# Values at the end of each unit, and a last token chunk filled up with zeros, in an attention + MLP-mixer kernel

## The chip, the core and the metric

The kernel runs on one NeuronCore of one Trainium2 chip. The metric is the device time of one execution in microseconds (us), as the median of several runs. Inputs and outputs lie in HBM. The engines work side by side, each through its own queue in program order: TensorE (matmuls, "PE"; its weight loads are "PEld"), VectorE ("DVE"), ScalarE ("ACT"), GpSimd ("POOL"), and SyncE ("SP"), which here only starts DMAs.

## What is computed

Threshold attention over 8 batches of 8 heads, 576 tokens and 64 dimensions per head, followed by one MLP-mixer block (mixing over tokens, then over channels) on the joined heads (576 x 512 per batch). All in float32; the four weights arrive as float64.

```python
# attention, per head
scores = q @ k.T / 8
thresh = max(scores, axis=-1) - tau
scores = where(scores >= thresh, scores, -1e9)
attn   = softmax(scores)                  # (sum + 1e-9)
x      = attn @ v                         # heads joined: (8, 576, 512)
# mixer
h   = relu(x.T @ w_tok1) @ w_tok2         # 576 -> 256 -> 576 tokens
u   = x + h.T
out = u + relu(u @ w_ch1) @ w_ch2         # 512 -> 1536 -> 512 channels
```

## The kernel before

The work on attention is cut into 144 units, 18 for each batch: one unit is 128 rows of scores for two heads (a pair). The 576 tokens are four chunks of 128 and a last one of 64; the last chunks of two pairs share a unit (`SHARED`). For one unit the steps are:

- `scores(u)`: TensorE multiplies with a contraction of 64 (the head's dimensions), head 0 in rows 0 to 63 of the array and head 1 in rows 64 to 127; VectorE takes the maximum; GpSimd makes the bias.
- `weigh(u)`: ScalarE makes the thresholded exponentials and their sums (four activations of 576 columns).
- `norm(u)`, one unit later: GpSimd divides by the sum.
- `turn...(u)`, two units later: transposed weights eT (on TensorE in batch 0; from batch 1 on by VectorE in 32x32 blocks and DMAs).
- `values(b, p, c)`: TensorE multiplies eT with v. Each head uses 64 columns of the array; the result is copied to xT by ScalarE.

```python
# scores: 64 rows of the array for each head
nc.tensor.matmul(sc[h][rows, f, 0:HS], lhsT=qT[r, cols], rhs=kT[r, HS*f : HS*f+HS], ...)   # r = 64 partitions
# values: 128 rows, 64 columns of the array for each head
nc.tensor.matmul(to[r], lhsT=vl[:, r], rhs=eT[:, NI], start=True, stop=False, ...)
for c in range(NI):
    for h in range(2):
        nc.tensor.matmul(to[r], lhsT=lv[:, j, :], rhs=eT[:, j], ...)
nc.scalar.copy(out=x, in_=ps)                            # to xT
```

Once the values of a batch are complete, `push(b)` puts the mixer's steps for it into a list (`todo`). `fill(share)` takes a share of a unit's quota from that list, so that TensorE has full-array work while the softmax of the units goes through the other engines. (`...` marks cuts.)

```python
def token_mlp(b):
    def turn_x(t):                                       # t = 0..4; MT = [128, 128, 128, 128, 64]
        M = MT[t]
        if t == 0:
            s["x"] = work.tile([P, NT, DM], F32, tag="x", bufs=1, ...)
        ...                                              # four transposes on TensorE
        nc.scalar.copy(out=s["x"][0:M, t, :], in_=...)
    def tok1(m):                                         # m = 0, 1
        for t in range(NT):
            M = MT[t]                                    # the last chunk: 64 rows
            nc.tensor.matmul(ps, lhsT=w1[0:M, t, P*m : P*m+P], rhs=s["x"][0:M, t, :], ...)
        nc.scalar.activation(out=s["a"][:, m, :], in_=ps, func=AF.Relu)
    def tok2(c, f): ...                                  # two matmuls; VectorE adds to xT
def channel_mlp(b, uT, i):
    def ch1(j): ...                                      # four matmuls "c", Relu to g on ScalarE
    def ch2(t, part): ...                                # transposes and three matmuls each, then out
```

The main loop, one turn for each unit. `weight(n)` prepares n steps of the mixer's weights (float64 to float32, on ScalarE, VectorE and GpSimd), as long as there are any.

```python
for u in range(len(units) + LAG + 4):
    ...
    if on: scores(u)
    if 0 < u <= len(units): norm(u - 1)
    if b_now: weight(2)
    if back: ...                                         # turn(w) or turn_blocks(w), w = u - 2; values become due
    if b_now: fill(0.4)
    weight(2 if b_now else 1)
    if on: weigh(u)
    if b_now: fill(0.3)
    while due and due[0][0] <= u:
        _, b, p, c = due.popleft()
        values(b, p, c)
        if p == NP - 1 and c == 1:
            push(b)
    if b_now: fill(0.3)
    weight(2 if b_now else 1)
    if on: ...                                           # loads of q, k, v; prep of later pairs
```

Each matmul of float32 operands in the program appears as two passes (two MATMUL records) in the trace.

Of the kernel before, what the change touches and what calls it, by code (L numbers as in the profile page):

```python
# [9 lines left out]
F32 = mybir.dt.float32  # L10
# [7 lines left out]
P = 128  # L18
# [3 lines left out]
def kernel(  # L22
# [26 lines left out]
    nc = tc.nc  # L49
    B, H, S, D = q.shape  # L50
    DM = H * D
# [3 lines left out]
    NI = 4  # L55
    MAIN = NI * P
    LAST = S - MAIN
    NT = NI + 1
    MT = [P] * NI + [LAST]
    NP = H // 2  # L60
# [8 lines left out]
    const = ctx.enter_context(tc.tile_pool(name="const", bufs=1))  # L69
    ld = ctx.enter_context(tc.tile_pool(name="ld", bufs=2))  # L70
    work = ctx.enter_context(tc.tile_pool(name="work", bufs=2))
# [52 lines left out]
    w1 = const.tile([P, NT, DTOK], F32, name="w1")  # L124
    w2 = const.tile([P, NTK, S], F32, name="w2")
    wc1 = const.tile([P, NJ, NCC, P], F32, name="wc1")
    wc2 = const.tile([P, NJ, DM], F32, name="wc2")

# [102 lines left out]
    def need(i):  # L233

        weight(3 * i + 4 - steps_done)
# [35 lines left out]
    def in_blocks(b):  # L271
        return b > 0

    def prep(n):
        lq, lk = loaded.pop(n)
        made = []
        for src, name in ((lq, "qT"), (lk, "kT")):
            sb = work.tile([P, S], F32, tag=name, name=f"{name}_{n}")
            nc.vector.transpose(out=sb, in_=src.rearrange("p n d -> p (n d)"))  # L279
            made.append(sb)  # L280
        heads[n] = made
# [99 lines left out]
    def values(b, p, c):  # L381

        lv, vl = vals[b * NP + p]
        if b not in xTs:
            xTs[b] = xTs[b + 1] = work.tile([P, NP, 2 * S], F32, tag="xT", name=f"xT_{b}")
        key = (b, p - p % 2, c) if c == "s" else (b, p, c)
        n, N, tok = (1, LAST, MAIN) if c == "s" else (2, 2 * P, 2 * P * c)
        first = LAST * (p % 2) if c == "s" else 0
        eT = eTs[key] if c == "s" else eTs.pop(key)
        if in_blocks(b):  # L390
            eT = eT[:, 0 : NK * n * P].rearrange("p (i c x) -> p c i x", i=4, c=NK)
            eT = eT[:, :, first // 32 : first // 32 + N // (32 * n), :]
        else:
            eT = eT[:, 0 : NK * n * P].rearrange("p (c x) -> p c x", c=NK)[:, :, first : first + N]
        ps = ps_tr.tile([P, MAIN], F32, tag="tr", name=f"pv_{b}_{p}_{c}")[:, 0:N]
        to = ps.rearrange("p (i x) -> p i x", x=32 * n) if in_blocks(b) else ps
        for h in range(2):
            r = slice(D * h, D * h + D)
            nc.tensor.matmul(to[r], lhsT=vl[:, r], rhs=eT[:, NI], start=True, stop=False, skip_group_check=True)  # L399
        for c in range(NI):  # L400
            for h in range(2):
                r = slice(D * h, D * h + D)
                j = (NI + 1) * h + c
                nc.tensor.matmul(to[r], lhsT=lv[:, j, :], rhs=eT[:, j], start=False, stop=(c == NI - 1), skip_group_check=True)  # L404
        x = xTs[b][:, p, S * (b % 2) + tok : S * (b % 2) + tok + N]
        if in_blocks(b) and n == 2:
            x = x.rearrange("p (n i x) -> p i n x", n=n, x=32)
            ps = ps.rearrange("p (i n x) -> p i n x", n=n, x=32)
        nc.scalar.copy(out=x, in_=ps)  # L409


    def token_mlp(b):
        xT = xTs.pop(b)
        o = S * (b % 2)
        s = {}

        def turn_x(t):
            M = MT[t]
            if t == 0:
                s["x"] = work.tile([P, NT, DM], F32, tag="x", bufs=1, name=f"x_{b}")  # L420
            ps = ps_tr.tile([P, MAIN], F32, tag="tr", name=f"tx_{b}_{t}").rearrange("p (c x) -> p c x", c=NP)
            for p in range(NP):
                nc.tensor.transpose(out=ps[0:M, p, :], in_=xT[:, p, o + t * P : o + t * P + M], identity=ident)  # L423
            nc.scalar.copy(out=s["x"][0:M, t, :], in_=ps[0:M].rearrange("q p d -> q (p d)"))

        def tok1(m):
            need(2)
            if m == 0:
                s["a"] = work.tile([P, NTK, DM], F32, tag="a", bufs=1, name=f"a_{b}")
            ps = ps_mm.tile([P, DM], F32, tag="mm", name=f"t1_{b}_{m}")  # L430
            for t in range(NT):
                M = MT[t]
                nc.tensor.matmul(ps, lhsT=w1[0:M, t, P * m : P * m + P], rhs=s["x"][0:M, t, :], start=(t == 0), stop=(t == NT - 1))  # L433
            nc.scalar.activation(out=s["a"][:, m, :], in_=ps, func=AF.Relu)

        def tok2(c, f):
            need(6)
            ps = ps_mm.tile([P, HS], F32, tag="mm", name=f"t2_{b}_{c}_{f}")
            for m in range(NTK):
                nc.tensor.matmul(  # L440
                    ps, lhsT=s["a"][:, m, P * c : P * c + P], rhs=w2[:, m, HS * f : HS * f + HS], start=(m == 0), stop=(m == NTK - 1)
                )
            u = xT[:, c, o + HS * f : o + HS * f + HS]
            nc.vector.tensor_add(out=u, in0=u, in1=ps)  # L444

        steps = [(0.44, lambda t=t: turn_x(t)) for t in range(NT)]
        steps += [(4.3, lambda m=m: tok1(m)) for m in range(NTK)]
        steps += [(0.97, lambda c=c, f=f: tok2(c, f)) for c in range(NCC) for f in range(2)]
        return steps
# [48 lines left out]
    def fill(share):  # L498
        nonlocal credit
        credit += share * quota  # L500
        while todo and credit > 0:
            cost, step = todo.popleft()
            credit -= cost
            step()
        if not todo:
            credit = 0.0

    def push(b):
        nonlocal quota
        uT = xTs[b]  # L510
        steps, old = token_mlp(b), list(todo)
        todo.clear()
        for i in range(max(len(steps), len(old))):
            todo.extend(old[i : i + 1])
            todo.extend(steps[i : i + 1])
        for i in range(2) if b % 2 == 0 else range(2, (2 * S + GR - 1) // GR):
            todo.extend(channel_mlp(b - b % 2, uT, i))
        quota = (sum(c for c, _ in todo) - (KEEP if b else 0.0)) / (UB - 1)

    prep(0)  # L520
    due = deque()
    b_now = 0
    LAG = 2
    for u in range(len(units) + LAG + 4):
        on = u < len(units)
        if u == UB:
            late.close()
            ps_mm = ctx.enter_context(tc.tile_pool(name="ps_mm", bufs=2, space=bass.MemoryType.PSUM))
        if on:
            b_now, p0, t = units[u]  # L530
            n = b_now * NP + p0
        w = u - LAG
        back = 0 <= w < len(units)
        if on:
            scores(u)
        if 0 < u <= len(units):
            norm(u - 1)
        if b_now:
            weight(2)
        if back:  # L540
            key, place, many = group_of(w)
            if in_blocks(key[0]):
                turn_blocks(w)
            else:
                for i in range(3):
                    turn(w, i)
            if place == many - 1:
                b, p, c = key
                if c == 0 and p % 2 == 0:
                    split_middle(b * NP + p)  # L550
                if c == "s":
                    split_middle(b * NP + p + 1)
                when = u + (2 if in_blocks(b) else 1)
                due += [(when, b, p + i, c) for i in range(2 if c == "s" else 1)]
        if b_now:
            fill(0.4)
        weight(2 if b_now else 1)
        if on:
            weigh(u)
        if b_now:  # L560
            fill(0.3)
        while due and due[0][0] <= u:
            _, b, p, c = due.popleft()
            values(b, p, c)
            if p == NP - 1 and c == 1:
                push(b)
        if b_now:
            fill(0.3)
        weight(2 if b_now else 1)
        if on:  # L570
            m = n + 2 + t // 4
            if t < 8 and m < len(pairs):
                load_qk(m, (nc.scalar if b_now else nc.sync,) * 2, t % 4)
                if t % 4 == 3:
                    load_v(m)
            if t == 2:
                prep(n + 1)
            if t == 7 and n + 2 < len(pairs):
                prep(n + 2)
    need(len(pieces) - 1)  # L580
    quota = 1e9
    fill(1.0)
# [28 lines left out]
```

## Time and profile before

| | before |
|---|---|
| median of 3 runs | 1413.92 us (1411.26 to 1416.02) |
| span of the profiled run | 1410.2 us |
| TensorE busy | 1338.3 us |
| VectorE, ScalarE busy | 585.2 us, 588.8 us |
| GpSimd busy | 358.9 us |
| mean granted TensorE clock | 0.984 |

How to read it: busy times are sums over the whole span. The page also cuts the span into 40 slices, each digit being the busy share in tenths; it lists the chain of work that ended last, groups of instructions by line of the kernel, and waits with what ended them. In rows of the timeline the columns are start (us), length (us), engine, line, operation, output<-inputs, shape of the array used (rows*columns), the moving operand and the number of passes. L297 is the scores, L399 and L404 the values, L423 the transposes of x, L433 the first token matmul (tok1), L440 the second, L462 and L478 the two channel matmuls.

### The profile page before, as it was taken

How to read it: one execution, taken by the hardware profiler on the slowest of the kernel's cores; microseconds unless marked ns; L12 is line 12 of the kernel's file. 1: busy time of each engine (PE TensorE's matmuls, PEld its weight loads, DVE VectorE, ACT ScalarE, POOL GpSimd, SP SyncE). 2: the span in 40 equal slices, each digit the busy share in tenths (PEclk: the TensorE clock that was granted, in tenths of full speed). 3: DMA queues.
4: the chain of work that ended last, by engine and by line, in shares of the span. 5: the costliest groups of instructions: out<-in, count | busy, mean ns of one | idle time of the engine just before them, and what ended most of it. 6: DMA issues, size and time to landing. Idle time of an engine off the chain costs nothing.

```text
span 1410.2 us, 19481 instructions
## 1 busy us (share of the span) xinstructions
PE 1338.3 (95%) x6866; PEld 828.3 (59%) x6866; DVE 585.2 (41%) x1009; ACT 588.8 (42%) x1328; POOL 358.9 (25%) x681
## 2 busy tenths in 40 slices
PE   5767799979999999999999999999999999999998
PEld 3443556536665567565756566565656466566675
DVE  5788673344444443434333444434333443201000
ACT  5776554344445444353334344443334344220110
POOL 4566552222222222222122222212212222100000
PEclk8998999989999999999999999999999999999999
DMA  6444654443444434433333434342443433300000
GB/s 133 103 104 115 170 136 110 106 101 92 118 117 105 107 87 101 104 93 93 90 95 83 111 81 116 91 109 68 99 94 77 111 90 79 88 8 16 8 8 23
DMA packets 257376, 128.34 MB, mean 91 GB/s; under 512 B 208064, under 2 KB 221376, under 8 KB 257280
## 3 DMA queue, kind: packets, MB, share of 16 engines
q1 hardware_dynamic: 131632, 111.46, 30.0%
q10 hardware_dynamic: 125648, 15.64, 7.0%
q8 instruction: 55, 0.90, 0.3%
q14 instruction: 41, 0.34, 0.1%
HBM read 43.25 MB, written 9.44 MB: 37 GB/s over the span
## 4 chain that ended last, share of the span: by engine, by line
PE 81%; DVE 6%; SPq 5%; DMA 3%; ACT 3%; issue 1%; POOL 1%; DVEq 0%; ACTq 0%
PE c L478 27%; PE c L462 23%; PE sc L297 10%; PE pv L404 7%; SPq L369 4%; PE t L433 4%; PE t L440 3%; DVE mx L302 3%; PE pv L399 2%; DVE T L359 2%; PE tx L423 1%; DMA eT<-T 1%; PE c L474 1%; ACT e L312 1%; ACT e L315 1%
## 5 line engine op out<-in xcount | busy, mean ns | idle before, releaser
L302 DVE TENSOR_REDUCE mx<-sc 128x1 f32<-128x576 f32 x288 | 204.7, 751 | 495.2 <-PE sc L297 493.2
L462 PE MATMUL c<-xT,wc 128*128 128x256 f32 (+1 forms) x1920 | 405.7, 363 | 3.1 <-ACT g L463 1.8
L478 PE MATMUL c<-wc,g 128*128 128x512 f32 x864 | 389.5, 597 | 0.0
L462 PEld LDWEIGHTS c<-xT,wc 128*128 128x128 f32 x1920 | 331.1, 190 | 76.9 <-issue 29.6
L303 POOL TENSOR_SCALAR bias<-mx,toff 128x1 f32<-128x1 f32 x288 | 79.6, 276 | 833.5 <-DVE mx L302 779.0
L312 ACT ACTIVATE e<-sc,bias 128x576 f32<-128x576 f32 x288 | 199.2, 740 | 168.3 <-POOL bias L303 156.3
L478 PEld LDWEIGHTS c<-wc,g 128*128 128x128 f32 x864 | 157.6, 190 | 177.3 <-issue 175.6
L463 ACT ACTIVATE g<-c 128x256 f32<-128x256 f32 (+1 forms) x240 | 86.9, 363 | 383.5 <-PE c L462 372.4
L325 POOL TENSOR_SCALAR e<-e,rr 128x576 f32<-128x576 f32 x288 | 219.6, 775 | 16.6 <-DVE rr L322 4.4
L315 ACT ACTIVATE e<-e,ntau 128x576 f32<-128x576 f32 x288 | 220.2, 772 | 0.0
L297 PE MATMUL sc<-kT,qT 64*128 64x288 f32 (+1 forms) x1280 | 191.9, 435 | 14.7 <-DVE kT L279 8.7
L359 DVE STREAM_TRANSPOSE T<-e 128x1152 f32<-128x1152 f32 x126 | 172.5, 1369 | 15.8 <-DMA eT<-T 10.0
L297 PEld LDWEIGHTS sc<-kT,qT 64*128 64x128 f32 (+1 forms) x1280 | 104.8, 179 | 95.7 <-issue 51.1
L404 PE MATMUL pv<-eT,lv 128*64 128x256 f32 x1024 | 125.8, 389 | 0.0
L483 DVE COPY o<-c 128x512 f32<-128x512 f32 x36 | 24.6, 684 | 192.6 <-PE c L478 192.6
L404 PEld LDWEIGHTS pv<-eT,lv 128*64 128x64 f32 x1024 | 76.5, 141 | 38.3 <-issue 2.8
L440 PE MATMUL t<-w,a 128*128 128x288 f32 x256 | 78.0, 434 | 13.9 <-DVE xT L444 12.1
L433 PE MATMUL t<-x,w 128*128 128x512 f32 (+1 forms) x160 | 74.9, 606 | 0.0
L409 ACT COPY xT<-pv 128x256 f32<-128x256 f32 x64 | 23.8, 372 | 115.1 <-PE pv L404 114.9
L440 PEld LDWEIGHTS t<-w,a 128*128 128x128 f32 x256 | 46.9, 197 | 38.4 <-DVE xT L444 17.0
L444 DVE TENSOR_TENSOR xT<-xT,t 128x288 f32<-128x288 f32 x64 | 27.9, 441 | 97.5 <-PE t L440 97.4
L315 ACT ACTIVATION_READ_ACCUMULATOR e<-e,ntau 128x1 f32 x288 | 57.0, 198 | 0.0
(46 smaller groups left out, 600.9 us busy)
## 6 DMA issues: line engine op xcount, KB each, us to landing
eT<-T SPq DMA_DIRECT2D x896, 72.0 KB, 2.1
scratch<-in_moe_w_ch_dram SPq DMA_DIRECT2D x24, 512.0 KB, 3.8
lv<-in_v_dram SPq DMA_DIRECT2D x32, 288.0 KB, 3.3
out_dram<-o SPq DMA_DIRECT2D x36, 256.0 KB, 2.2
eT<-T SPq DMA_DIRECT2D x224, 36.0 KB, 1.9
lk<-in_k_dram ACTq DMA_DIRECT2D x108, 72.0 KB, 2.7
lq<-in_q_dram ACTq DMA_DIRECT2D x104, 72.0 KB, 2.1
lq<-in_q_dram SPq DMA_DIRECT2D x24, 72.0 KB, 3.3
```

Of the source, the lines that this page charges most:

```text
L297: nc.tensor.matmul(sc[h][rows, f, 0:HS], lhsT=qT[r, cols], rhs=kT[r, HS * f : HS * f + HS], start=True, stop=True)
L302: nc.vector.tensor_reduce(out=mx[:, c], in_=sc[h][:, :, 0:HS], axis=AX.XY, op=ALU.max)
L312: nc.scalar.activation(out=eh, in_=sc[h][:, :, 0:HS], func=AF.Prelu, bias=bias[:, h : h + 1], scale=SCALE, alpha=STEEP)
L315: nc.scalar.activation(out=eh, in_=eh, func=AF.Exp, bias=ntau, accum_out=rs[:, h : h + 1])
L325: nc.gpsimd.tensor_scalar(out=eh, in0=eh, scalar1=rr[:, h : h + 1], scalar2=1.0, op0=ALU.mult, op1=ALU.mult)
L359: nc.vector.transpose(out=T.rearrange("p (a c n x) -> p c a n x", a=4, c=NK, n=n)[:, :, :, place, :], in_=e.rearrange("p (c a x) -> p c a ...
L404: nc.tensor.matmul(to[r], lhsT=lv[:, j, :], rhs=eT[:, j], start=False, stop=(c == NI - 1), skip_group_check=True)
L433: nc.tensor.matmul(ps, lhsT=w1[0:M, t, P * m : P * m + P], rhs=s["x"][0:M, t, :], start=(t == 0), stop=(t == NT - 1))
L440: nc.tensor.matmul(ps, lhsT=s["a"][:, m, P * c : P * c + P], rhs=w2[:, m, HS * f : HS * f + HS], start=(m == 0), stop=(m == NTK - 1))
L462: nc.tensor.matmul(ps, lhsT=wc1[:, j, c, :], rhs=uT[:, c, GR * i : GR * i + n], start=(c == 0), stop=(c == NCC - 1))
L463: nc.scalar.activation(out=s["g"][:, j, 0:n], in_=ps, func=AF.Relu)
L478: nc.tensor.matmul(flat, lhsT=s["g"][:, j, P * t : P * t + P], rhs=wc2[:, j, :], start=False, stop=(j == NJ - 1), skip_group_check=True)
```

## The change

It does two things. The `values` of a unit are emitted at the end of the loop's turn, after all three parts of the fill and after weight steps and loads, so that the scores of the next unit follow them directly on TensorE. And the last chunk of 64 tokens in tok1 is multiplied at 128 rows: x gets a fixed buffer whose rows 64 to 127 of the last chunk are set to zero once, and so are those rows of w1. Both are meant to keep together what uses TensorE in the same shape.

```diff
@@ constants
+    x_sb = const.tile([P, NT, DM], F32, name="x_sb")
+    nc.gpsimd.memset(x_sb[LAST:P, NI, :], 0.0)
+    nc.gpsimd.memset(w1[LAST:P, NI, :], 0.0)
@@ turn_x
-            if t == 0:
-                s["x"] = work.tile([P, NT, DM], F32, tag="x", bufs=1, name=f"x_{b}")
...
-            nc.scalar.copy(out=s["x"][0:M, t, :], in_=ps[0:M].rearrange("q p d -> q (p d)"))
+            nc.scalar.copy(out=x_sb[0:M, t, :], in_=ps[0:M].rearrange("q p d -> q (p d)"))
@@ tok1
-                M = MT[t]
-                nc.tensor.matmul(ps, lhsT=w1[0:M, t, P * m : P * m + P], rhs=s["x"][0:M, t, :], ...)
+                nc.tensor.matmul(ps, lhsT=w1[:, t, P * m : P * m + P], rhs=x_sb[:, t, :], ...)
@@ main loop
         if b_now:
-            fill(0.3)
-        while due and due[0][0] <= u:
-            _, b, p, c = due.popleft()
-            values(b, p, c)
-            if p == NP - 1 and c == 1:
-                push(b)
-        if b_now:
-            fill(0.3)
+            fill(0.6)
         weight(2 if b_now else 1)
         if on:
             ...                                          # loads, prep
+        while due and due[0][0] <= u:
+            _, b, p, c = due.popleft()
+            values(b, p, c)
+            if p == NP - 1 and c == 1:
+                push(b)
```

More of the change, by code (lines that the diff above doesn't have):

```diff
@@ L431, in tok1 @@
             for t in range(NT):
-                M = MT[t]
-                nc.tensor.matmul(ps, lhsT=w1[0:M, t, P * m : P * m + P], rhs=s["x"][0:M, t, :], start=(t == 0), stop=(t == NT - 1))
+                nc.tensor.matmul(ps, lhsT=w1[:, t, P * m : P * m + P], rhs=x_sb[:, t, :], start=(t == 0), stop=(t == NT - 1))
             nc.scalar.activation(out=s["a"][:, m, :], in_=ps, func=AF.Relu)
```

## The prediction

> **What bounds the kernel now.** I read the page first: busy time, the 40 slices, the chain. Columns of the first line: busy us, share of the span, instructions; a slice is 35.3 us.
>
> ```profile
> PE 1338.3 (95%) x6866; PEld 828.3 (59%) x6866; DVE 585.2 (41%) x1009; ACT 588.8 (42%) x1328; POOL 358.9 (25%) x681
> PE   5767799979999999999999999999999999999998
> DVE  5788673344444443434333444434333443201000
> PE 81%; DVE 6%; SPq 5%; DMA 3%; ACT 3%; issue 1%; POOL 1%; DVEq 0%; ACTq 0%
> ```
>
> TensorE is full from about slice 6 to the end; the first five slices (0 to 175 us: batch 0, and the start of batch 1 while weights are still being prepared) are a second stage in which VectorE is busier and TensorE waits. Next, the waits of TensorE alone, from 160 us on. Columns: total us, times, longest us.
>
> ```profile
> PE t L440 <- DVE xT L444: 7.7, 7, 2.9
> PE pv L399 <- DMA eT<-T: 5.0, 2, 4.2
> PE sc L297 <- ACT e L312: 3.3, 2, 2.0
> ```
>
> With three smaller rows that is 20 us of waits in 1250 us. So in the main stage nothing is to be had from waits: only from what TensorE itself spends. A large busy share does not say that this is all arithmetic, so I read the timeline of TensorE by the START of each row (an end is only modelled). One unit of batch 1:
>
> ```profile
> 180.59 0.65 PE L399 MATMUL pv<-eT,vl 128*64 128x256 f32 x4
> 181.07 1.90 PE L404 MATMUL pv<-eT,lv 128*64 128x256 f32 x16
> 182.90 1.99 PE L462 MATMUL c<-xT,wc 128*128 128x256 f32 x8
> 184.82 1.24 PE L297 MATMUL sc<-kT,qT 64*128 64x288 f32 x8
> 185.99 3.72 PE L462 MATMUL c<-xT,wc 128*128 128x256 f32 x16
> ```
>
> The 8 passes of c between values (pv) and scores (sc) take 184.82 - 182.90 = 1.92 us. Near the end, where c stands between work of its own shape, and tok1 (L433) between two c:
>
> ```profile
> 1257.56 1.99 PE L462 MATMUL c<-xT,wc 128*128 128x256 f32 x8
> 1259.39 4.65 PE L433 MATMUL t<-x,w 128*128 128x512 f32 x10
> 1263.97 1.99 PE L462 MATMUL c<-xT,wc 128*128 128x256 f32 x8
> 1265.80 1.13 PE L440 MATMUL t<-w,a 128*128 128x288 f32 x4
> 1266.77 1.89 PE L462 MATMUL c<-xT,wc 128*128 128x256 f32 x8
> 1268.49 1.13 PE L440 MATMUL t<-w,a 128*128 128x288 f32 x4
> ```
>
> Here the same 8 passes take 1268.49 - 1266.77 = 1.72 us (0.215 each). So a stretch of full-array work placed between pv and sc costs 0.20 us more than its passes. The starts of single passes show where: the last pass before a change of shape (128x128, 128x64, 64x128) is followed after 309 ns instead of 216, or 522 instead of 429 for 512 columns (+93); and the second pass after the change comes 104 ns late (320 for 216, 533 for 429), 51 ns where the new weights have 64 columns (260 for 209), 57 where the stretch begins with 128-wide transposes. The tok1 row hides the same thing: its last two passes, the chunk of 64 tokens, have 64 rows. The ten passes of 0.429 should take 4.29; it takes 1263.97 - 1259.39 = 4.58, and the c after it takes 1259.39 - 1257.56 = 1.83, 0.11 over its 1.72. Together 0.40 us lost per tok1 between full-array work.
>
> **What the Trainium skill says.** "TensorEngine Tiling (Array Packing)", section Tiling Modes, Key Properties: changing the tiling mode, and not merely the tile, drains TensorE. The trace agrees: +93 ns at each change, none between L440 and L462, and none at the 64-column transposes of the last chunk. "TensorE: Matmul & The Clock Gate", section LDWEIGHTS, gives a weight load as columns / 1.2 ns: an estimate from that page is 107 ns for 128 columns and 53 for 64. The trace's 104 and 51 ns after a change look like one load that is no longer hidden; that this is the cause is my reading. "Perfetto Trace Analysis", section Tensor Engine Instruction, says that a matmul's end is estimated; hence the starts.
>
> **The change, part by part.**
>
> (a) Values move behind the third part of the fill. In the order of the two programs on TensorE (before running anything) I counted stretches of equal shape, from the first transpose of x on. Before: 70 stretches of values, of which 49 are followed by full-array work and 21 by scores. After: 70, of which 3 are followed by full-array work (in the tail, where no scores are left) and 67 by scores. So 46 full-array stretches vanish: their passes join the ones before. Each saves one drain and one exposed load, 0.20 us, except that about 8 of them begin with transposes and save 0.15: 46 x 0.20 - 8 x 0.05 = 8.8 us. The number of matmuls is unchanged, and pv still pays its own change to sc. In batch 0 values already stood next to scores; nothing there.
>
> (b) The last chunk at 128 rows, zeros in both operands. The passes cost the same (a pass of 512 columns takes 0.429 whatever its rows). 16 tok1 steps. What follows them in the order before: full-array work 3 times, values 8, scores 5. Between full-array work it saves 0.40: 3 x 0.40 = 1.2. Where a change comes next anyway, only entry and load vanish, 0.195: 8 x 0.195 = 1.6. With scores of the same 64x128 mode next, the trace shows scores slipped between the two 64-row passes (a score starts 13 ns after the first one at 470.04 us); from there to the end of the scores takes 2.02 us, and without sharing I get 0.429 + 0.522 + 1.17 = 2.12, less the entry of 0.09 that goes: nothing, for 4 of the 5; the fifth has 64x64 scores and saves 0.2. Sum (b) 3.0 us. Added: two memsets on GpSimd in the first microseconds. From the row of the 128x128 memset, 205 ns each, I take some 0.5 us, beside the first loads: 0.
>
> (c) The order around the end of a batch. Values of the last pair now come after the weight steps, and the new batch's token steps are handed out after that. In the order, the scores of unit 21 stand ahead of the transposes of x (tx), before behind them:
>
> ```profile
> 120.08 0.66 PE L423 MATMUL tx<-ident,xT 128*128 128x128 f32 x4
> 127.22 3.76 PE L423 MATMUL tx<-ident,xT 128*128 128x128 f32 x16 [6.48 <-ACT xT L409]
> 130.91 1.79 PE L297 MATMUL sc<-kT,qT 64*128 64x288 f32 x8
> ```
>
> The 1.7 us of scores now fall into that 6.48 us wait, as soon as exp's first step has released their PSUM (about 125 us), and their maximum reaches VectorE sooner; VectorE sat idle 1.41 us for this one and 2.92 us for the next. Against it: ScalarE now does two weight steps (0.66 + 0.65 us) ahead of the copy of xT that tx waits for, and one more after it. The same exchange comes at the next boundary (unit 40, near 300 us); there tx waited for nothing, so I count nothing. I put the net of (c) at 2 us gained, with an uncertainty of 4 to either side, since this stage is a mesh of short waits.
>
> **Sum.** 8.8 + 3.0 + 2 = 13.8. 1413.9 - 13.8 = 1400.1; I say 1400. All of (a) and (b) lies in a stage where TensorE hardly waits, so nearly all of it should reach the end.
>
> **The rivals.**
>
> R1, the pass-through fails: a new wait takes the place. Channel-mixing steps now stand in one block of about 6 us per unit, and c has two PSUM buffers which ScalarE empties behind four activations of 0.75 us. If c waited there for 1 us in each of the 46 units, the change would cost 46 us less 12: 1448. Against it: in units without values the block is uninterrupted already, and from 160 us on c waited for g once, 1.8 us. I expect under 3 us.
>
> R2, values later in the unit are values too late: xT, then tx and tok1, slip by a third of a unit's fill, 2 us at each of 8 batches. If TensorE had nothing else, 16 us would cancel the gain: 1416. For it: the two boundaries in (c), where the queue of work is empty. Against it: from batch 2 on 45 us of older steps are kept back for exactly this, and no wait of tx is listed after 160 us. What does move to the good side: pv waited 5.0 us for eT by DMA, and now has 0.3 of a fill more.
>
> R3, the drains are hidden time anyway, or an entry into scores costs more straight after values than after full-array work. Then (a) gives little: 1410. Against it: where values already stood next to scores, pv to sc shows the same 309 ns and the same 347 ns for the first pair of scores as after full-array work.
>
> **Range and chances.** (a) and (b) are counts times measured gaps: 11.8 +- 1. The run-to-run spread of the times (1411.3 to 1416.0) and (c) make most of the range: 1394 to 1406. Faster by over 2% needs 28 us, more than twice the switches and beyond the 20 us of waits put together: 3%. Slower by over 2% needs R1 almost in full: 1%.
>
> **What would show each step.** Right: the timeline has sc directly behind pv at pv's start + 2.3 us; the L433 rows with 64 rows are gone and ten passes start 0.429 apart throughout; TensorE's busy time falls by about 12 us; waits from 160 us on stay near 20 us. Wrong: c waiting for g (R1), tx for xT (R2), or the first pair of scores after pv slower than 347 ns (R3). The prediction fails if the first 340 us alone move by over 6 us, since there my sum is least worked out.

## The result and the profile after

The changed kernel takes 1401.9 us (median of 6 runs, 1398.7 to 1404.0); the kernel before, measured beside it, 1414.8 us (6 runs, 1411.3 to 1416.8). The ratio is 0.9907, with a 95% interval of 0.9888 to 0.9927: 13.2 us less, between 10.3 and 15.8. Foretold were 1400 us and a gain of 13.8.

In the changed kernel the lines are: L301 scores, L403 and L408 values, L425 transposes of x, L434 tok1, L441 the second token matmul ("tok2" below), L445 VectorE's addition after it, L463 and L479 the channel matmuls. From the page after, the lines that answer to those of before:

```profile
PE 1332.0 (95%) x6866; PEld 833.3 (59%) x6866; DVE 585.6 (42%) x1009; ACT 589.1 (42%) x1328; POOL 359.1 (26%) x683
PE   5776899989999999999999999999999999999998
DVE  5689674445444443434333444434333444201000
PE 83%; DVE 7%; SPq 3%; ACT 2%; DMA 2%; POOL 1%; issue 1%; DVEq 0%; ACTq 0%; POOLq 0%
```

The number of matmul passes is the same (6866), no other engine works less, and TensorE is still the bound. Its busy time is 6.3 us lower here and 11.0 lower in the second trace of the same kernel (1327.3; run e12 below); about 12 were foretold. Passes at half the granted clock count as busy for longer (16 passes of values took 2.73 us at 47 us here, 1.90 at 45 us in the second trace), and the two traces have different amounts of them, so busy time measures such changes badly.

The timeline of TensorE after, one unit of batch 1 and the two tok1 of the last batch:

```profile
178.11 5.45 PE L463 MATMUL c<-xT,wc 128*128 128x256 f32 x24
183.49 0.65 PE L403 MATMUL pv<-eT,vl 128*64 128x256 f32 x4
183.97 1.90 PE L408 MATMUL pv<-eT,lv 128*64 128x256 f32 x16
185.80 1.24 PE L301 MATMUL sc<-kT,qT 64*128 64x288 f32 x8
186.97 3.72 PE L463 MATMUL c<-xT,wc 128*128 128x256 f32 x16
```

```profile
1245.40 4.45 PE L434 MATMUL t<-x_sb,w 128*128 128x512 f32 x10
1249.69 1.89 PE L463 MATMUL c<-xT,wc 128*128 128x256 f32 x8
1251.42 4.46 PE L434 MATMUL t<-x_sb,w 128*128 128x512 f32 x10
1255.71 1.89 PE L463 MATMUL c<-xT,wc 128*128 128x256 f32 x8
```

The scores start 185.80 - 183.49 = 2.31 us after the values, just as long as values took before, and the eight passes of c that stood between them are now at the end of a block of 24. tok1 takes 1249.69 - 1245.40 = 4.29 us instead of 4.58, and the c after it 1.73 instead of 1.83: the 0.40 us are gone.

The waits of TensorE from 160 us on:

```profile
PE t L441 <- DVE xT L445: 10.1, 9, 2.8
PE pv L403 <- DMA eT<-T: 2.1, 1, 2.1
PE c L463 <- ACT g L464: 2.0, 1, 2.0
PE sc L301 <- ACT e L316: 2.0, 1, 2.0
```

Their sum with three smaller rows is 20.1 us, as before (20.4). The first row went from 7.7 to 10.1, but near 160 us this depends on which side of the border a wait falls: in the second trace the row is 7.3. From 340 us on the two traces agree within 0.1 us, and the mixer's matmuls wait longer than before. Before:

```profile
PE t L440 <- ACT g L463: 1.8, 5, 0.4
PE t L440 <- DVE xT L444: 1.6, 4, 0.5
PE c L462 <- DVE xT L444: 0.8, 1, 0.8
```

and after:

```profile
PE t L441 <- DVE xT L445: 4.1, 6, 0.8
PE t L441 <- ACT g L464: 1.8, 5, 0.4
PE c L463 <- DVE xT L445: 1.7, 2, 0.8
```

These rows show only a part: a wait that falls under the modelled end of the pass before it is listed as shorter than it is. So I made a table from the starts alone. A stretch is a run of passes in one array shape; its excess is the time from its first start to the first start of the next stretch, less passes times steady gap (429 ns for 512 columns, 215.5 for 256, 242.5 for 288 and so on). "Inside" is the part of the full-array excess that is not at its ends. All from 340 us on, in us:

| kernel | full-array stretches | their excess | of it inside | scores' excess | values' excess | 64-row tok1 | sum of excess |
|---|---|---|---|---|---|---|---|
| before | 141 | 38.3 | 10.4 | 22.2 | 8.5 | 0.5 | 69.6 |
| after | 101 | 34.0 | 14.3 | 19.6 | 8.4 | - | 61.9 |
| e1, move alone | 103 | 34.4 | 14.3 | 20.4 | 8.4 | 1.1 | 64.3 |
| e2, zeros alone | 138 | 37.6 | 10.4 | 20.8 | 8.9 | - | 67.3 |
| e4, mirror | 99 | 31.1 | 10.5 | 19.9 | 8.2 | - | 59.3 |
| e9, tok2 PSUM after | 101 | 21.4 | 1.8 | 19.6 | 8.4 | - | 49.4 |
| e10, tok2 PSUM before | 141 | 32.2 | 4.3 | 22.3 | 8.8 | 0.5 | 63.8 |

Before to after, 40 stretches went and took (38.3 - 10.4) - (34.0 - 14.3) = 8.2 us with them, 0.205 us each. But 3.9 us came back inside the remaining ones. Of the scores' 2.6 us, 1.2 are two pauses of 0.6 us that only the old order of values has (its scores at 810.41 us take 1.80 us to the next start instead of 1.17, and so do those at 1136.71); the rest only changes columns, since scores had shared three 64-row stretches of tok1. The second trace of the changed kernel gives the same sums within 0.1 us.

### The profile page after: what moved, and what is told of

It reads as the page before. It is cut to its first block, busy times and chain, and to the rows that moved or that the text cites. A ratio compares the mean times of both kernels' runs of the same rounds, so it can differ in the third digit from the quotient of the medians.

```text
span 1401.9 us, 19510 instructions
## 1 busy us (share of the span) xinstructions
PE 1332.0 (95%) x6866; PEld 833.3 (59%) x6866; DVE 585.6 (42%) x1009; ACT 589.1 (42%) x1328; POOL 359.1 (26%) x683
## 4 chain that ended last, share of the span: by engine, by line
PE 83%; DVE 7%; SPq 3%; ACT 2%; DMA 2%; POOL 1%; issue 1%; DVEq 0%; ACTq 0%; POOLq 0%
PE c L479 27%; PE c L463 24%; PE sc L301 11%; PE pv L408 7%; PE t L434 4%; PE t L441 3%; DVE mx L306 3%; PE pv L403 2%; SPq L373 2%; DVE T L363 2%; PE tx L425 1%; PE c L475 1%; PE pv_s L408 1%; DMA scratch<-in_moe_w_ch_dram 1%; ACT e L316 1%
## 5 line engine op out<-in xcount | busy, mean ns | idle before, releaser
L463 PE MATMUL c<-xT,wc 128*128 128x256 f32 (+1 forms) x1920 | 401.7, 362 | 4.1 <-ACT g L464 2.0
L479 PE MATMUL c<-wc,g 128*128 128x512 f32 x864 | 388.9, 596 | 0.0
L463 PEld LDWEIGHTS c<-xT,wc 128*128 128x128 f32 x1920 | 332.8, 190 | 75.2 <-issue 27.2
L479 PEld LDWEIGHTS c<-wc,g 128*128 128x128 f32 x864 | 157.8, 190 | 177.8 <-issue 176.3
L301 PE MATMUL sc<-kT,qT 64*128 64x288 f32 (+1 forms) x1280 | 192.3, 439 | 18.6 <-ACT e L316 9.7
L301 PEld LDWEIGHTS sc<-kT,qT 64*128 64x128 f32 (+1 forms) x1280 | 104.5, 181 | 95.8 <-issue 47.7
L408 PE MATMUL pv<-eT,lv 128*64 128x256 f32 x1024 | 127.0, 392 | 0.0
L408 PEld LDWEIGHTS pv<-eT,lv 128*64 128x64 f32 x1024 | 76.6, 142 | 40.0 <-issue 5.4
L441 PE MATMUL t<-w,a 128*128 128x288 f32 x256 | 76.2, 426 | 12.2 <-DVE xT L445 10.1
L434 PE MATMUL t<-x_sb,w 128*128 128x512 f32 x160 | 73.4, 606 | 0.0
L441 PEld LDWEIGHTS t<-w,a 128*128 128x128 f32 x256 | 46.4, 194 | 35.9 <-DVE xT L445 15.2
L445 DVE TENSOR_TENSOR xT<-xT,t 128x288 f32<-128x288 f32 x64 | 28.0, 441 | 76.8 <-PE t L441 76.7
```

The source lines that it names most:

```text
L434: nc.tensor.matmul(ps, lhsT=w1[:, t, P * m : P * m + P], rhs=x_sb[:, t, :], start=(t == 0), stop=(t == NT - 1))
L441: nc.tensor.matmul(ps, lhsT=s["a"][:, m, P * c : P * c + P], rhs=w2[:, m, HS * f : HS * f + HS], start=(m == 0), stop=(m == NTK - 1))
L463: nc.tensor.matmul(ps, lhsT=wc1[:, j, c, :], rhs=uT[:, c, GR * i : GR * i + n], start=(c == 0), stop=(c == NCC - 1))
L479: nc.tensor.matmul(flat, lhsT=s["g"][:, j, P * t : P * t + P], rhs=wc2[:, j, :], start=False, stop=(j == NJ - 1), skip_group_check=True)
```

## The experiments

Theory: what counts is the number of stretches of equal array shape; each costs a drain and an exposed weight load. The rivals: the gain is in ScalarE's and the softmax's timing at batch boundaries; the changes of shape are hidden anyway; the later values cost something back. Times are medians; ratios are to the kernel before, measured beside the experiment, with their 95% intervals. Its median differs between the sets of runs (1411.8 to 1414.8 us), so the difference of two medians from two sets can be off by 3 us; where it matters, the difference by the two ratios stands beside it.

**e1: the move alone**

```diff
 # the changed kernel's main loop; turn_x and tok1 as before (64 rows for the last chunk)
```

> The move of values alone, the last chunk back at 64 rows. Theory (each stretch of equal array shape costs a drain and an exposed weight load, 0.20 us): the order has 46 full-array stretches fewer than before, so 9 us less plus what the start of batch 1 brings: 1403 to 1406, ratio to before 0.992 to 0.994. Rival (the gain of the change is that ScalarE and the softmax run ahead at batch boundaries): the gain comes in the first 350 us and the drift after that is flat.

1404.5 us, ratio 0.9939 (0.9921 to 0.9957): 8.6 us less. In the table its stretches fall from 141 to 103, and the sum of the excess by 5.3 us from 340 us on. Between unit 43 (330 us) and unit 138 (1164 us) its scores gain 5.3 us on those of before, so the rival that puts the whole gain into the first 350 us falls. Its lead at unit 43 is 3.8 us, more than the eight stretches that vanish ahead of 340 us explain (1.6).

**e2: the zeros alone**

```diff
 # the changed kernel's x_sb, memsets, turn_x and tok1; main loop as before
```

> The last chunk at 128 rows alone, values in the old place. Theory: 12 of 16 tok1 steps save 0.195 us or 0.40 us, 4 save nothing because scores had shared the 64-row stretch: 3 us less, 1411 to 1413, ratio 0.997 to 0.999. Rival (128 rows cost more than 64, or the shared stretches had been worth more than the drains): 1414 to 1418.

1407.5 us, ratio 0.9968 (0.9956 to 0.9980): 4.5 us less, between 2.8 and 6.2. The 3 us foretold lie inside; the median is below the range given, 1411 to 1413, in part because the kernel before took 1412.0 here and not 1414.8. From 340 us on the sum of the excess is 2.3 us lower. By unit 43 the scores are already 3.4 us ahead, more than the four tok1 there can give (0.4 each at most); what else came there stays open. The two experiments together make 13.1 us, the change itself 13.2: its parts add up.

**e4: values directly behind the next unit's scores**

```diff
-    for u in range(len(units) + LAG + 4):
+    for u in range(len(units) + LAG + 5):                # one turn more, for the last values
...
         if on:
             scores(u)
+        while due and due[0][0] <= u - 1:
+            ...  # values, push, as in the changed kernel
@@ end of the turn
-        while due and due[0][0] <= u:
-            ...
```

> The mirror of the change: values directly behind the scores of the next unit instead of ahead of them. The order has 315 changes of shape against 314, the same 3 stretches per unit, but values come later by one scores. Theory (the number of stretches counts, not which comes first): within 3 us of the changed kernel, 1399 to 1405. Rival (what matters is that scores reach VectorE early, or that xT is late): scores come a values' time (2.2 us) earlier and xT later, so the time differs from the changed kernel by over 5 us.

1387.1 us, ratio 0.9826 (0.9805 to 0.9847): nearly twice the change's gain. The theory of stretches alone does not give that. Where it comes from is seen in the starts of the scores. From unit 43 to unit 138 the mirror gains 8.5 us on before and the changed kernel 6.9; at unit 43 the mirror is already 18.5 us ahead of before, 15.0 ahead of the second trace of the changed kernel. (Up to 2.3 us of such a lead is the order itself, since its scores start ahead of the values.) Up to 160 us, TensorE waits for VectorE's copies of eT, in the changed kernel:

```profile
PE tr L352 <- DVE eT L354: 16.9, 9, 3.0
PE pv L403 <- DVE eT L354: 2.7, 4, 0.9
```

and in the mirror:

```profile
PE tr L352 <- DVE eT L354: 8.5, 6, 3.1
```

There is no row for the values there. In batch 0 the eT of the values is copied out of PSUM by VectorE just before they run. Values ahead of scores wait for that copy and keep the scores waiting too; behind scores, no such wait is listed, and scores, on which the maximum and all that follows depends, come earlier. The larger part is the transposes (tr), which wait for VectorE half as long; that this comes from the earlier scores is my reading, and no run separates it. So of the two orders that save the same number of changes, the one taken leaves time on the table where TensorE is not the bound. The mirror's row in the table also has 10.5 us inside its stretches, not 14.3, and a sum 2.6 us lower than the changed kernel's.

**e7: the mirror for batch 0 alone**

```diff
+        # behind scores(u): values with due[0][1] == 0 (batch 0), due one turn later
-        while due and due[0][0] <= u:
+        while due and due[0][1] > 0 and due[0][0] <= u:
```

> The changed kernel, with the values of batch 0 alone behind the scores of the next unit. Theory A (the mirror's further 15 us came from batch 0 and the first units of batch 1, where scores no longer stand behind values that wait for eT): all of it here, 1386 to 1391. Theory B (it came from the main stage, values behind scores being better everywhere): 1398 to 1403. If half and half, 1392 to 1396.

1395.0 us, ratio 0.9877 (0.9855 to 0.9898): 6.9 us less than the changed kernel by the medians, 4 by the two ratios, about half of what the mirror gains on it (14.8 and 11). Against the second trace of the changed kernel its scores are 4.4 us earlier at unit 20, 7.2 at unit 24 and 7.6 at unit 43, and stay there; those of e4 are 5.0, 11.8 and 15.0 earlier. So theory A had the place right (nearly all before unit 43), but batch 0 alone gives half of it: the rest comes with the values of batch 1, in units 22 to 42. What they wait for there stays open.

**e5: each values cut in two by a full-array step**

```diff
         for c in range(NI):
+            if c == 1 and todo:
+                cost, step = todo.popleft()
+                credit -= cost
+                step()
             for h in range(2):
```

> The changed kernel with each values cut in two by one full-array step of the list of mixer steps. The same matmuls; the order has 82 values stretches and 82 full-array stretches more. Theory: 82 x (0.20 + 0.145) = 28 us more than the changed kernel, 1426 to 1432. Rival (changes of shape are hidden behind other work, the gain came from elsewhere): within 6 us of the changed kernel, 1396 to 1408.

1450.2 us, ratio 1.0266 (1.0248 to 1.0284): 48 us more than the changed kernel, not 28. The rival of hidden changes falls, but the dose had a side effect: the extra step is taken whether or not the unit's quota allows it, and the next unit gets less. Its scores then come before ScalarE has emptied their PSUM. In the waits of the weight loads from 340 us on:

```profile
PEld sc L301 <- ACT e L316: 20.2, 30, 2.4
```

In the changed kernel that row is 0.4 us. The scores' excess from 340 us on is 30.5 us instead of 19.6.

**e6: the same cut, within the unit's share**

```diff
-            fill(0.6)
+            fill(0.3 if due and due[0][0] <= u else 0.6)
@@ values
         for c in range(NI):
+            if c == 1 and b_now and second:   # second: not for the second of two 64-token values
+                fill(0.3)
```

> The dose again without its side effect: values cut in two by a part of the unit's own fill (0.3 ahead of it, 0.3 inside), so that no unit gets more or less mixer work than in the changed kernel. The order has 53 values stretches and 53 full-array stretches more. Theory: 53 x (0.20 + 0.145) = 18 us more than the changed kernel, 1416 to 1423, and no more waits of scores for ScalarE than there. Rival (the first dose's 48 us were the price of the changes themselves, 0.58 us each pair): 31 us more, 1430 to 1436.

1417.8 us, ratio 1.0037 (1.0022 to 1.0052): 15.9 us more than the changed kernel's median, or 18 by the two ratios (1.0037 / 0.9907 = 1.013), for 18 foretold. The wait of the weight loads of the scores for ScalarE is back at 0.4 us, so the side effect is gone. One such unit in the timeline:

```profile
701.74 0.65 PE L403 MATMUL pv<-eT,vl 128*64 128x256 f32 x4
702.23 0.60 PE L410 MATMUL pv<-eT,lv 128*64 128x256 f32 x4
702.76 1.99 PE L465 MATMUL c<-xT,wc 128*128 128x256 f32 x8
704.68 1.52 PE L410 MATMUL pv<-eT,lv 128*64 128x256 f32 x12
706.13 1.24 PE L301 MATMUL sc<-kT,qT 64*128 64x288 f32 x8
```

The eight passes of c take 704.68 - 702.76 = 1.92 us again, as they did between values and scores before the change, and the two parts of values 1.02 + 1.45 = 2.47 us instead of 2.31. The cost of a stretch holds as a dose: taken away it gains, added it costs.

**e8: values directly after the fill, ahead of weight steps and loads**

```diff
             fill(0.6)
+        # values, push here
         weight(2 if b_now else 1)
         if on: ...
-        # values, push here
```

> The changed kernel with values emitted directly after the fill, ahead of the weight steps and loads. The order on TensorE is the same; on ScalarE the copy of xT stands ahead of the weight steps again. Theory: the copy's place matters only at the first batch boundary, where tx waited for x_sb behind weight steps: 1 to 3 us less, 1398 to 1402. Rival (ScalarE's order around the copy is part of the gain): 1404 to 1410.

1401.2 us, ratio 0.9913 (0.9893 to 0.9933): the same as the changed kernel. The place of ScalarE's copy of xT among the weight steps is worth nothing that can be measured. The rival's loss does not show; the number lies in the theory's range, but so does no difference at all.

**e9: tok2 in another PSUM pool**

```diff
-            ps = ps_mm.tile([P, HS], F32, tag="mm", ...)
+            ps = ps_tr.tile([P, MAIN], F32, tag="tr", ...)[:, 0:HS]
```

> The changed kernel with the second token matmul's output in the pool of the transposes' PSUM instead of the two buffers shared with the channel matmul. From 340 us on the full-array stretches lose 13.8 us within themselves beyond their changes of shape, against 10.1 before the change, most of it at channel to token matmul. Theory (that is the wait for a PSUM buffer that VectorE empties): it falls by 4 us or more, 1393 to 1399. Rival (the wait is for something else, such as the operand a, or for the pool's other users): within 2 us of the changed kernel, 1400 to 1404.

1388.1 us, ratio 0.9824 (0.9802 to 0.9845): 13.8 us less than the changed kernel by the medians, 12 by the two ratios, about three times the 4 foretold. Inside the full-array stretches 1.8 us are left of 14.3. The wait, in the timeline of TensorE of the changed kernel:

```profile
808.19 1.14 PE L441 MATMUL t<-w,a 128*128 128x288 f32 x4
809.16 1.05 PE L463 MATMUL c<-xT,wc 128*128 128x128 f32 x8
811.00 1.24 PE L441 MATMUL t<-w,a 128*128 128x288 f32 x4 [0.79 <-DVE xT L445]
```

and the same work in e9:

```profile
800.94 1.14 PE L441 MATMUL t<-w,a 128*128 128x288 f32 x4
801.91 1.05 PE L463 MATMUL c<-xT,wc 128*128 128x128 f32 x8
802.80 1.14 PE L441 MATMUL t<-w,a 128*128 128x288 f32 x4
```

The eight passes of c take 811.00 - 809.16 = 1.84 us in the first, 0.89 in the second: 0.95 us were lost, of which the bracket lists 0.79. The mixer's two PSUM buffers go by turns to t and c, so each t waits until VectorE has added the t before it to xT. What e9 shows is the price of sharing the two buffers: it leaves both to c and tok1, and all three waits listed above (7.6 us together, 5.8 for VectorE and 1.8 for ScalarE's g) are gone, so it does not tell the engines apart. VectorE's timeline, at the like place of an earlier batch of the changed kernel, shows what that addition stands behind:

```profile
482.20 1.42 DVE L306 TENSOR_REDUCE mx<-sc 128x1 f32<-128x576 f32 x2 [6.00 <-PE sc L301]
483.54 0.16 DVE L325 TENSOR_SCALAR rr<-rs 128x2 f32<-128x2 f32 x1
483.73 0.17 DVE L326 RECIPROCAL rr<-rr 128x2 f32<-128x2 f32 x1
484.14 1.38 DVE L363 STREAM_TRANSPOSE T<-e 128x1152 f32<-128x1152 f32 x1 [0.24 <-POOL bias L307]
485.44 0.42 DVE L445 TENSOR_TENSOR xT<-xT,t 128x288 f32<-128x288 f32 x1
```

The unit's maximum and transpose, 2.8 us in VectorE's order, come ahead of a 0.42 us addition.

**e10: the same on the kernel before**

```diff
 # the kernel before, with e9's line for tok2
```

> The kernel before, with the second token matmul's output in the transposes' PSUM, nothing else. In the traces from 340 us on, full-array stretches lost 10.4 us inside themselves before the change and 14.3 after it, and the other pool took 12.5 of those 14.3. Theory (the wait was there before and the change made it longer by some 4 us): it gains less here than on the changed kernel, 9 to 11 us against 13.8, so 1402 to 1405, and on top of it the change brings 14 to 17 us instead of 13. Rival (the change made no difference to that wait): the same gain, 13 to 15 us, 1398 to 1400.

1407.5 us, ratio 0.9957 (0.9938 to 0.9975): 6.1 us less, not 9 to 11, and in the table 10.4 goes to 4.3. So the wait was there before and smaller: the other pool takes away 6.1 us inside the stretches of the kernel before and 12.5 in the changed one. The cause of the 4.3 us left stays open. With the other pool on both sides the change brings 19 us (1407.5 to 1388.1) instead of 13.

**e11: mirror and PSUM together**

```diff
 # e4 with e9's line for tok2
```

> Values behind the next unit's scores, the last chunk with zeros, and the second token matmul in the transposes' PSUM. If the two gains have separate causes they add up: 25 us of the mirror and 14 of the PSUM, less what the mirror had already taken from the second (its stretches lost 10.5 us inside themselves, not 14.3): 1375 to 1380. If the mirror's values, now next to scores at the start of a unit, keep the same PSUM busy when the token matmuls want it: 1383 to 1388.

1379.2 us, ratio 0.9767 (0.9745 to 0.9790): 33 us less than before, two and a half times the change's gain. Against e4 the PSUM brings 8 us, where 8.9 us are missing inside the stretches (10.5 to 1.6): the gains have separate causes and nearly add up. It is the fastest version here.

**e12: the changed kernel again**

```diff
 # no edit
```

> The changed kernel once more, for a second trace. In the first trace its scores of unit 10 start 3.6 us later than before the change, though the order of TensorE's work in batch 0 is the same. Theory (that is the phase of TensorE's clock in the first 50 us, as variants with the same order start unit 10 between 0.3 and 1.1 us later): here unit 10 starts within 2 us of before, and the span is 1396 to 1400. Rival (the later copy of xT in batch 0 costs it): again 3 to 4 us late.

One run, 1402.7 us, with a span of 1400.5. Its scores of unit 10 start 0.5 us later than before the change, not 3.6. In the first trace the 16 passes of values at 34 us took 3.63 us and those at 47 us 2.73; at the same places of the order they took 3.23 and 1.90 in the kernel before, 3.40 and 1.90 in the second trace. So 3 us of difference in the first 50 us are not the kernel's, and passes at half clock account for most of them; the span is within 0.5 us of the range expected.

## Why the prediction was right, and where it was not

**(a) Moving values: the price of a stretch was right, a wait took part of it back.** I put 8.8 us on 46 vanished stretches. From 340 us on, 40 vanished with the whole change, 38 with the move alone (e1), and the 40 took 8.2 us with them (8.0 by my 0.20 us each); e6 shows the same cost when stretches are added. But the sentence "nearly all of it should reach the end" failed: inside the full-array stretches 3.9 us came back, at the PSUM buffers that tok2 and the channel matmul share (by e9 and e10 that wait grew from 6.1 to 12.5 us, and the rest inside fell). This was R1 in another place. I looked for it at the channel matmul and ScalarE, where it stayed small (c waited for g 2.0 us, once; 3.6 us in the second trace), and not at tok2 and VectorE, which my list of waits showed in its first row. Why it grew is argued, not shown: before, values stood inside the fill and gave VectorE 2.3 us to come to the addition, and e4, whose values stand at the head of the fill, has 10.5 us of it as before.

**(b) The zeros: right in size.** 3.0 us foretold, 4.5 (2.8 to 6.2) measured alone. From 340 us on, where 12 of the 16 tok1 stand, 2.3 us of excess went. Scores had slipped between the two 64-row passes in three of the four cases counted so, not in the one at 310.77 us.

**(c) The batch boundaries: a gain, smaller than its uncertainty.** Up to unit 44 (340 us) the second trace of the changed kernel gains 3.0 us on before, counted from unit 10, the first 4.8. About 2 of these belong to (a) and (b) in batch 1 (46 - 38 = 8 stretches of 0.2 us, and four tok1). So (c) is near 1 us in one trace and near 3 in the other, which neither confirms the 2 nor refutes it, and e8 shows no part of the copy's place in it. The scores of unit 21 did fall into the wait, as I said; what I did not say is the next line of the timeline after: tx waited for ScalarE's copy to x_sb.

```profile
126.52 2.76 PE L301 MATMUL sc<-kT,qT 64*128 64x288 f32 x8 [3.62 <-ACT e L316]
129.21 1.88 PE L425 MATMUL tx<-ident,xT 128*128 128x128 f32 x8
134.96 2.85 PE L425 MATMUL tx<-ident,xT 128*128 128x128 f32 x12 [3.87 <-ACT x_sb L426]
```

One wait of 6.48 us became two, of 3.62 and 3.87, in this trace.

**The sum.** 8.8 + 3.0 + 2 = 13.8 against 13.2 (10.3 to 15.8). The parts measured from 340 us on, 69.6 - 61.9 = 7.7 us, and 3.0 ahead of it make 10.7 in the traces. The profiled run of before was itself 2.8 us faster than its median (1412.0 against 1414.8), which is about the gap. The total came out closer than its steps, and in part by luck: 3.9 us that I did not foresee were lost inside the stretches, 1.2 that I did not foresee were gained at the scores, and the interval is wide enough for both.

**The rivals.** R2 (later values delay the mixer) did not come: tx waited 0.4 us from 160 us on. R3 fell: the first pair of scores takes 347 ns after values and after full-array work, before and after the change. R1 came at another matmul, at a twelfth of its size.

## What to carry to other kernels

When TensorE is full, count the stretches of equal array shape in its order and price one from the starts of two like runs in the timeline; putting those of the odd shapes next to each other costs no matmul. Then ask which of the orders that save the same number keeps the producer of the longest chain (here the scores) from standing behind something that waits. And a PSUM buffer that a busy engine empties late can hide among busy rows: measure start to start, because the list of waits counts only what sticks out beyond a modelled end.

## What the runs showed of the hardware

- A change of array shape costs twice: 93 to 100 ns at the last pass before it, and 104 ns (128 columns of new weights) or 51 (64 columns) at the second pass after it. A full-array stretch between two others costs 0.20 us, values 0.145, scores 0.20, the same whether 128x64 meets 64x128 or either meets 128x128, and the same in all traces within some ns.
- A 64-row pass of tok1 and scores, which use 64 rows too, ran side by side without the 93 ns between them: in the kernel before, at 470.04 us, the scores' first pass started 13 ns after the tok1 pass.
- Filling up 64 rows to 128 with zeros cost no time: ten passes of 512 columns take 4.29 us then, 0.429 each. With 64 rows in the last two, two of the gaps between starts were 522 and 533 ns instead of 429, which is the two costs of a change.
- In the first 50 us the granted clock falls to half for a few us, at places that differ between two traces of one kernel: it is 0.50 from 45.4 to 48.8 us in the first and 1.00 from 43 to 48 us in the second (16 passes of values there: 2.73 us and 1.90). Unit 10 starts 3 us apart in them.
